# Grouped-query decode attention on one core: the second of the last four value pieces loaded by five loads of 112, 5, 5, 3 and 3 partitions in place of one of 128

## The chip, the core and the metric

The kernel runs on one core of one Trainium2 chip. Its time is the device time of one execution in microseconds (us). The kernel before takes 628.2 us, the median of three runs that lie between 628.05 and 628.32 us. The engines are named as in the profile: PE is TensorE (PEld its weight loads), DVE VectorE, ACT ScalarE, POOL GpSimd and SP SyncE. SP does no arithmetic here; it issues the loads. Behind it stand the core's 16 DMA engines, which carry the bytes. In this document "engine" alone, where loads are spoken of, means one of those 16.

## The reference

Thirty-two query heads attend to 65,536 keys; four query heads share one of eight key and value heads. There is one query per head and the head size is 128, all in bf16:

```python
B, Hq, Hkv, Sq, Sk, D = 1, 32, 8, 1, 65536, 128

def reference(q, k, v):
    rep = Hq // Hkv
    k = jnp.repeat(k, rep, axis=1)
    v = jnp.repeat(v, rep, axis=1)
    scale = D ** -0.5
    scores = jnp.einsum("bhqd,bhkd->bhqk", q, k) * scale
    p = _softmax(scores, axis=-1)
    return jnp.einsum("bhqk,bhkd->bhqd", p, v)
```

Keys and values are 134 MB each, and every byte is used once.

## The kernel before

**Tiling.** The key and value rows of a head are cut into two halves, so there are 16 rounds (NR) of 8 MB of keys and 8 MB of values. In a round, each of the 128 partitions holds 256 row tiles of 128 numbers (2T = 256), so that one load of a whole round's values has 128 rows of 64 KB. `vbuf` holds one round's values. A round is computed in two parts, of A = 160 and C = 96 row tiles.

**The compute loop.** PE turns each key tile (line 139), DVE or ACT copies eight of them out of PSUM (lines 246 and 248), and PE multiplies them by the queries into scores (line 157). DVE takes the largest score, POOL spreads it over the partitions, ACT makes the exponentials (line 416), and PE multiplies them by the value tiles (`stretch`, line 183): one matmul a row tile, accumulated in PSUM. In an odd round, `stretch` runs over the row tiles in the order 96 to 159 (`q` = 1), 160 to 255 (`q` = 2) and 0 to 95 (`q` = 0). The rescaling of the running sums is done on DVE (lines 319 and 322).

**The loads.** SP issues all loads of keys and values on one queue in the order of use: keys of a round when `kfree` says that the key buffer is free, values when `vfree` does. A whole round's load is one DMA, and its completion adds 16 to a semaphore. The loop in the middle loads one DMA for keys and one for values a round. The last round is cut finer, so that PE can begin before all of it has landed: its keys come in three loads, and its values in five. First come row tiles 96 to 255 (semaphore `vrdy[0]`), then row tiles 0 to 95 in four pieces of 62, 22, 9 and 3 row tiles (`V_PIECES`), each with a semaphore of its own in `vpiece`. These four are the "last four value pieces".

**The waits on them.** In `stretch` with `q` = 0 the matmul that starts a piece (row tiles 0, 62, 84 and 93) waits for its semaphore. That code is one loop for all rounds, so the waits are also met in the earlier rounds, where the pieces don't exist: SP adds 16 to each of the four at the start, no wait takes anything off, and SP takes the 16 off again just ahead of the last round's value loads.

**The end.** After the last matmul of the last stretch, DVE adds the partial sum (line 322), PE turns the sum (line 215), DVE and ACT divide it (lines 402 and 439), and SP stores the last head's four rows (line 517). The other 28 rows are stored a little earlier by ACT's queue (line 438).

Of the kernel before, what the change touches and what calls it, by code (L numbers as in the profile page):

```python
# [10 lines left out]
P = 128  # L11
# [13 lines left out]
HU = 4  # L25

V_PIECES = (62, 22, 9, 3)

LOOP_SLOT = 0

# [11 lines left out]
def take(e, sem, n=1):  # L42

    e.wait_ge(sem, n)
    e.sem_inc(sem, -n)  # L45


def bass_standalone__gqa_softmax__decode_kernel(nc, q, k, v, out):
# [14 lines left out]
    def row_tile(odd, x):  # L63
        return (x + C) % (2 * T) if odd else x
# [6 lines left out]
    def sb(name, shape, dt):  # L71
        return S(nc.sbuf_tensor(name, shape, dt))

    def sem(name):
        return S(nc.semaphore(name))

    kbuf = sb("kbuf", [P, (2 * T + C) * D], DT.bfloat16)
    vbuf = sb("vbuf", [P, 2 * T * D], DT.bfloat16)
# [38 lines left out]
    vrdy = [sem(f"vrdy{i}") for i in range(2)]  # L117
    vpiece = [sem(f"vpiece{i}") for i in range(len(V_PIECES))]
    kfree, vfree = sem("kfree"), sem("vfree")
# [59 lines left out]
    def stretch(pe, q):  # L179
        a, b = ((0, C), (C, A), (A, 2 * T))[q]  # L180
        starts = [sum(V_PIECES[:n]) for n in range(len(V_PIECES))] if q == 0 else []
        for r in range(a, b):
            ins = pe.matmul(vsum[q], lhsT=vbuf[:, r * D:(r + 1) * D], rhs=pts[:, r * R:(r + 1) * R],  # L183
                            start=r == a, stop=r == b - 1)
            if r in starts:
                ins.wait_op(vpiece[starts.index(r)], 16, "sem-ge")
        return ins

    def pe_values(pe, n):

        with pe.If(n > 0):
            take(pe, vrdy[0], 16)
            take(pe, exd)
            stretch(pe, 1)


        odd = (n + 1) % 2  # L200
        with pe.Fori(odd, 2) as s:
            with pe.If(n > 0):
                with pe.If(s > 0):
                    take(pe, vrdy[1], 16)
                    take(pe, exd)
                    stretch(pe, 2).then_inc(pvd, 1)
            with pe.If(n > 0):
                with pe.If((n + 1 + s) % 2 < 1):
                    take(pe, exd)
                    stretch(pe, 0).then_inc(pvd, 1)  # L210
# [248 lines left out]
    def pairs(x):  # L459

        return x.rearrange("h (c p t) d -> (h c) p (t d)", c=HALVES, p=P)

    def sync_engine(e):
        kp, vp = pairs(kf), pairs(vf)

        def cols(a, b):
            return slice(a * D, b * D)

        def load_k(i, odd, split=(0,)):

            for n, f in enumerate(split):
                last = (split + (len(K_PARTS),))[n + 1]
                a, b = K_PARTS[f], (K_PARTS + (2 * T,))[last]
                r = row_tile(odd, a) if b - a < 2 * T else 0
                t = r if odd else C + r
                e.dma_start(kbuf[:, cols(t, t + b - a)], kp[i][:, cols(r, r + b - a)]).then_inc(krdy[f], 16)
                for x in range(f + 1, last):
                    e.sem_inc(krdy[x], 16)

        def load_v(i, ready, a, b):  # L480
            e.dma_start(vbuf[:, cols(a, b)], vp[i][:, cols(a, b)]).then_inc(ready, 16)

        def load_both(i, odd):
            take(e, kfree)
            load_k(i, odd)
            take(e, vfree)
            load_v(i, vrdy[0], 0, 2 * T)
            e.sem_inc(vrdy[1], 16)

        load_k(0, 0, (0, 1, 2))  # L490
        load_v(0, vrdy[0], 0, 2 * T)

        for sm in [vrdy[1]] + vpiece:
            e.sem_inc(sm, 16)
        load_both(1, 1)
        with e.Fori(1, H - 1) as h:
            load_both(2 * h, 0)
            load_both(2 * h + 1, 1)
        i = NR - 2
        take(e, kfree)  # L500
        load_k(i, 0, (0, 2))
        take(e, vfree)
        load_v(i, vrdy[0], 0, A)
        load_v(i, vrdy[1], A, 2 * T)
        i = NR - 1
        take(e, kfree)
        load_k(i, 1, (0, 1, 2))
        take(e, vfree)
        for sm in vpiece:
            e.sem_inc(sm, -16)  # L510
        load_v(i, vrdy[0], C, 2 * T)
        e.sem_inc(vrdy[1], 16)
        r = 0
        for n, sm in zip(V_PIECES, vpiece):
            load_v(i, sm, r, r + n)
            r += n
        ins = e.dma_start(of[HR - R:HR, :].rearrange("(a b) d -> a b d", a=2), olast[:, :])
        ins.wait_op(t_last, 2, "sem-ge")
        ins.then_inc(o_sem, 16)
# [4 lines left out]
    scalar_engine(nc.scalar)  # L524
    gpsimd_engine(nc.gpsimd)
    sync_engine(nc.sync)
    nc.sync.wait_ge(o_sem, 32)
    es.close()
# [27 lines left out]
```

## Time and profile before

| | |
|---|---|
| median of three runs | 628.2 us (628.05 to 628.32) |
| the profiled execution, as timed | 628.48 us |
| its span, first to last instruction | 627.2 us |
| granted TensorE clock, mean over the span | 0.768 |
| HBM read | 268.44 MB |
| busy: PE, DVE, ACT, POOL | 78%, 45%, 38%, 3% |

The span is what the profile's rows are placed in; the 1.3 us between it and the 628.48 us lie around the first and the last instruction. Times in the rows are microseconds from the span's start, unless they are marked ns. A row of the timeline reads: start, duration, engine, line, operation, what is written from what, and how many instructions were merged into it. In a table of windows, each row is a stretch of time with the busy time of every engine, the count of instructions in brackets, the granted clock, the busy share of the 16 DMA engines and the rate.

### The profile page before, as it was taken

The page shows a single profiled execution, that of the slowest core. Times are in us where ns is not written, and L with a number is a line of the kernel's source. Part 1 is how long each engine was busy: PE and PEld are TensorE (multiplying, and loading weights), DVE is VectorE, ACT ScalarE, POOL GpSimd, SP SyncE. Part 2 cuts the span into 40 slices and gives each one's busy share as a digit, 9 for nine tenths or more (in the row PEclk, how much of TensorE's full clock was granted, in tenths as well). Part 3 has the DMA queues.
Part 4 walks back from the last instruction along what each step waited for, and adds up shares of the span by engine and source line. Part 5 has one row for each costly group of instructions (what it writes and reads, how often), then busy time and mean ns, then how long its engine had stood idle before and what let it go on. Part 6 is the DMA issues. An engine that isn't in the chain of part 4 may idle for free. (4 is left out here: it accounts for less than half of the span.)

```text
span 627.2 us, 27062 instructions
## 1 busy us (share of the span) xinstructions
PE 486.8 (78%) x12291; PEld 482.8 (77%) x12291; DVE 284.0 (45%) x667; ACT 235.5 (38%) x467; POOL 16.4 (3%) x49
## 2 busy tenths in 40 slices
PE   1873994959859498695976959679496895989898
PEld 1873985959859498694966959679496895989897
DVE  2530553616546065361734617345173552736365
ACT  1330441524425044251533515335052351624354
POOL 0000000000000000000000000000000000000000
PEclk9975875858769587695966959678596785958697
DMA  9999999999999999999999999999999999999997
GB/s 368 439 442 431 435 435 435 431 426 443 426 443 426 439 426 439 426 435 431 431 439 431 439 431 431 439 431 439 431 431 439 431 439 431 412 436 425 432 438 303
DMA packets 6155, 268.59 MB, mean 428 GB/s; under 512 B 770, under 2 KB 898, under 8 KB 1154
## 3 DMA queue, kind: packets, MB, share of 16 engines
q1 hardware_dynamic: 6056, 268.44, 99.2%
q8 instruction: 7, 0.11, 0.1%
q10 hardware_dynamic: 90, 0.02, 0.0%
q14 instruction: 2, 0.02, 0.0%
HBM read 268.44 MB, written 0.01 MB: 428 GB/s over the span
## 5 line engine op out<-in xcount | busy, mean ns | idle before, releaser
L139 PE MATMUL trb<-ident,kbuf 128*128 128x128 bf16 x4096 | 299.8, 236 | 111.3 <-PEq L45 105.3
L139 PEld LDWEIGHTS trb<-ident,kbuf 128*128 128x128 bf16 x4096 | 268.1, 107 | 112.6 <-issue 111.6
L246 ACT ACTIVATE ktb<-trb 128x1024 bf16<-128x1024 bf16 x176 | 180.1, 1023 | 352.2 <-PE trb L139 345.2
L248 DVE COPY ktb<-trb 128x1024 bf16<-128x1024 bf16 x336 | 221.3, 689 | 170.1 <-PE trb L139 167.3
L157 PE MATMUL qkb<-qcur,ktb 128*128 128x4 bf16 x4096 | 132.1, 164 | 0.0
L157 PEld LDWEIGHTS qkb<-qcur,ktb 128*128 128x128 bf16 x4096 | 124.2, 96 | 0.0
L183 PE MATMUL pvb<-pts,vbuf 128*128 128x4 bf16 x2560 | 71.8, 166 | 11.2 <-PEq L45 11.2
L183 PEld LDWEIGHTS pvb<-pts,vbuf 128*128 128x128 bf16 x2560 | 70.0, 102 | 13.1 <-issue 13.1
L416 ACT ACTIVATE pts<-qkb,negm 128x160 bf16<-128x160 f32 (+1 forms) x128 | 51.9, 548 | 0.0
L283 DVE TENSOR_REDUCE cmax<-qkb 128x4 f32<-128x640 f32 (+1 forms) x32 | 22.1, 691 | 58.8 <-DVEq L45 58.8
L183 PE MATMUL qkb<-pts,vbuf 128*128 128x4 bf16 x1536 | 43.4, 166 | 4.5 <-PEq L45 4.5
L183 PEld LDWEIGHTS qkb<-pts,vbuf 128*128 128x128 bf16 x1536 | 42.4, 104 | 5.0 <-issue 5.0
L416 ACT ACTIVATION_READ_ACCUMULATOR pts<-qkb,negm 128x1 f32 x128 | 34.2, 267 | 0.0
L455 POOL PARTITION_ALL_REDUCE cmaxa<-cmax x32 | 12.0, 375 | 578.0 <-POOLq L45 578.0
L410 ACT ACTIVATE alpha<-dm 128x4 f32<-128x4 f32 x32 | 6.4, 201 | 31.9 <-ACTq L45 31.9
L333 DVE COPY acc<-qkb 128x4 f32<-128x4 f32 x8 | 1.3, 162 | 35.3 <-DVEq L45 35.3
L311 DVE TENSOR_TENSOR lp<-lp,alpha 128x4 f32<-128x4 f32 x24 | 3.9, 162 | 26.8 <-DVEq L45 26.8
L322 DVE TENSOR_TENSOR acc<-acc,pvb 128x4 f32<-128x4 f32 x32 | 5.0, 158 | 22.8 <-DVEq L45 22.0
L223 PE MATMUL trb<-ident,qsb 32*128 32x32 bf16 x1 | 0.2, 179 | 11.5 <-issue 11.5
L223 PEld LDWEIGHTS trb<-ident,qsb 32*128 32x128 bf16 x1 | 0.1, 101 | 11.5 <-issue 11.5
L300 DVE TENSOR_TENSOR m<-m,cmaxa 128x4 f32<-128x4 f32 x24 | 3.8, 159 | 8.8 <-DVEq L45 8.8
L319 DVE TENSOR_TENSOR acc<-acc,alpha 128x4 f32<-128x4 f32 x24 | 3.9, 162 | 4.2 <-DVEq L45 3.7
(45 smaller groups left out, 38.1 us busy)
## 6 DMA issues: line engine op xcount, KB each, us to landing
kbuf<-in_k_dram SPq DMA_DIRECT2D x5, 3072.0 KB, 24.4
vbuf<-in_v_dram SPq DMA_DIRECT2D x2, 5120.0 KB, 22.4
kbuf<-in_k_dram SPq DMA_DIRECT2D x1, 5120.0 KB, 18.6
kbuf<-in_k_dram SPq DMA_DIRECT2D x2, 2048.0 KB, 12.8
vbuf<-in_v_dram SPq DMA_DIRECT2D x1, 3072.0 KB, 27.6
vbuf<-in_v_dram SPq DMA_DIRECT2D x1, 1984.0 KB, 28.3
vbuf<-in_v_dram SPq DMA_DIRECT2D x1, 704.0 KB, 29.6
vbuf<-in_v_dram SPq DMA_DIRECT2D x1, 288.0 KB, 29.9
```

The lines of the kernel that those rows point to most:

```text
L139: ins = pe.transpose(trb[j % NTB][:, i * P:(i + 1) * P], kbuf[:, t * D:(t + 1) * D], ident[:, :])
L157: ins = pe.matmul(bank[:, t * R:(t + 1) * R], lhsT=ktb[:, off:off + P], rhs=qcur[:, :], start=True, stop=True)
L183: ins = pe.matmul(vsum[q], lhsT=vbuf[:, r * D:(r + 1) * D], rhs=pts[:, r * R:(r + 1) * R], start=r == a, stop=r == b - 1)
L246: ins = e.activation(dst, trb[j % NTB][:, :], AF.Copy).then_inc(eva, 1)
L248: ins = e.tensor_copy(dst, trb[j % NTB][:, :]).then_inc(evd, 1)
L283: e.tensor_reduce(cmax[:, :], qkb[part][:, 0:n * R].rearrange("p (t g) -> p g t", g=R), AX.X, ALU.max).then_inc(cm, 1)
L311: chain(e, lambda: e.tensor_tensor(lp[:, :], lp[:, :], alpha[u % 2][:, :], ALU.mult), lambda: e.tensor_tensor(lp[:, :], lp[:, :], rsum[u % ...
L319: return lambda: e.tensor_tensor(acc, acc, alpha[u % 2][:, :], ALU.mult)
L322: return lambda: e.tensor_tensor(acc, acc, vsum[q], ALU.add)
L410: e.activation(alpha[u % 2][:, :], dm[u % 2][:, :], AF.Exp, scale=scale)
L416: ins = e.activation(pv[:, g, r:r + n], sv[:, g, 0:n], AF.Exp, bias=negm[b][:, g:g + 1], scale=scale, accum_out=rsum[b][:, g:g + 1])
L455: e.partition_all_reduce(cmaxa[:, :], cmax[:, :], P, bass.bass_isa.ReduceOp.max).then_inc(cma, 1)
```

## The change

The second piece, 22 row tiles of all 128 partitions, is loaded by five DMAs that share its semaphore: partitions 0 to 111, 112 to 116, 117 to 121, 122 to 124 and 125 to 127. Each adds 16 when it is complete, so that this piece's semaphore stands at 80 when all have landed (`landed`). PE's wait for the piece is for 80, and SP's additions at the start and subtraction before the last round are 80 for it as well. The other three pieces, their order and the bytes are as before.

```diff
 V_PIECES = (62, 22, 9, 3)
+SHARED = 1
+ROWS = ((0, 112), (112, 117), (117, 122), (122, 125), (125, 128))
+
+
+def landed(n):
+    return 16 * (len(ROWS) if n == SHARED else 1)
...
             if r in starts:
-                ins.wait_op(vpiece[starts.index(r)], 16, "sem-ge")
+                ins.wait_op(vpiece[starts.index(r)], landed(starts.index(r)), "sem-ge")
...
-        def load_v(i, ready, a, b):
-            e.dma_start(vbuf[:, cols(a, b)], vp[i][:, cols(a, b)]).then_inc(ready, 16)
+        def load_v(i, ready, a, b, rows=slice(0, P)):
+            e.dma_start(vbuf[rows, cols(a, b)], vp[i][rows, cols(a, b)]).then_inc(ready, 16)
...
-        for sm in [vrdy[1]] + vpiece:
-            e.sem_inc(sm, 16)
+        e.sem_inc(vrdy[1], 16)
+        for n, sm in enumerate(vpiece):
+            e.sem_inc(sm, landed(n))
...
-        for sm in vpiece:
-            e.sem_inc(sm, -16)
+        for n, sm in enumerate(vpiece):
+            e.sem_inc(sm, -landed(n))
         load_v(i, vrdy[0], C, 2 * T)
         e.sem_inc(vrdy[1], 16)
         r = 0
-        for n, sm in zip(V_PIECES, vpiece):
-            load_v(i, sm, r, r + n)
+        for x, (n, sm) in enumerate(zip(V_PIECES, vpiece)):
+            for a, b in ROWS if x == SHARED else ((0, P),):
+                load_v(i, sm, r, r + n, slice(a, b))
             r += n
```

On SP's queue, at the end of its program, the values of the last round stood so before (the size is partitions by numbers in a row; 2816 numbers are the 22 row tiles of the second piece):

```order
L481 DMA vbuf<-in_v_dram 128x20480
L481 DMA vbuf<-in_v_dram 128x7936
L481 DMA vbuf<-in_v_dram 128x2816
L481 DMA vbuf<-in_v_dram 128x1152
L481 DMA vbuf<-in_v_dram 128x384
L517 DMA out_dram<-olast 4x128
```

and stand so now:

```order
L487 DMA vbuf<-in_v_dram 128x20480
L487 DMA vbuf<-in_v_dram 128x7936
L487 DMA vbuf<-in_v_dram 112x2816
L487 DMA vbuf<-in_v_dram 5x2816 x2
L487 DMA vbuf<-in_v_dram 3x2816 x2
L487 DMA vbuf<-in_v_dram 128x1152
L487 DMA vbuf<-in_v_dram 128x384
L525 DMA out_dram<-olast 4x128
```

Four DMAs are new, and the third and fourth pieces are issued behind them. On PE, the last stretch of value matmuls keeps its order and its four waiting instructions; the first row names the wait for the vectors of exponentials and the first piece:

```order
L189 MATMUL qkb<-pts,vbuf 128x4 [waits exd,vpiece0]
L189 MATMUL qkb<-pts,vbuf 128x4 x61
L189 MATMUL qkb<-pts,vbuf 128x4 [waits vpiece1]
L189 MATMUL qkb<-pts,vbuf 128x4 x21
L189 MATMUL qkb<-pts,vbuf 128x4 [waits vpiece2]
L189 MATMUL qkb<-pts,vbuf 128x4 x8
L189 MATMUL qkb<-pts,vbuf 128x4 [waits vpiece3]
L189 MATMUL qkb<-pts,vbuf 128x4 x2
```

These rows read as before but for the line number; only the value waited for at `vpiece1` is another.

## The prediction

> **What bounds the kernel now.** I read the page's counters first, then the chain that ended last, then the last five microseconds in windows.
>
> ```profile
> span 627.2 us, 27062 instructions
> ...
> DMA  9999999999999999999999999999999999999997
> ...
> DMA packets 6155, 268.59 MB, mean 428 GB/s; under 512 B 770, under 2 KB 898, under 8 KB 1154
> ...
> q1 hardware_dynamic: 6056, 268.44, 99.2%
> q8 instruction: 7, 0.11, 0.1%
> q10 hardware_dynamic: 90, 0.02, 0.0%
> ```
>
> The queue of the loads keeps the 16 DMA engines busy for 99.2% of the span, and in all forty slices but the last. So the kernel is bound by its loads, and the change neither adds a byte nor moves one before the last round. Only two things can change the time: when the last bytes land, and how much work is left behind them.
>
> The chain of waits, in order of time, shows what is left:
>
> ```profile
> 619.53 0.04 issue
> 619.58 2.70 PE pvb L183 x96
> 622.28 2.79 PE qkb L183 x96
> 625.07 0.02 issue
> 625.09 0.17 DVE acc L322
> ```
>
> It starts at 619.53 us and is PE's two last stretches, without a stop that the chain would name. PE's own timeline gives the second stretch from its first start, and the table of windows the clock:
>
> ```profile
> 622.16 2.89 PE L183 MATMUL qkb<-pts,vbuf 128*128 128x4 bf16 x96
> ...
> 619.60:620.60 1.00, 1.00 (x39) 1.00 (x40) 0.00 (x0) 0.93 (x6) 0.00 (x0) 0.50 0.94 395
> ...
> 623.20:624.20 1.00, 1.00 (x43) 1.00 (x41) 0.67 (x5) 0.00 (x0) 0.00 (x0) 0.50 0.33 119
> ```
>
> The same 96 matmuls at the same granted clock of 0.50 take 2.70 us in the stretch whose values had long landed and 2.89 us in the one that waits for the four pieces. So 2.89 - 2.70 = 0.19 us is all that the pieces cost PE now. That they cost anything is seen in the issues and their landings (SP's timeline, then the list of issues, whose last number is the time from issue to landing):
>
> ```profile
> 594.14 0.42 SPq L481 DMA_DIRECT2D vbuf<-in_v_dram  x1
> ...
> 594.62 0.90 SPq L481 DMA_DIRECT2D vbuf<-in_v_dram  x2
> ```
>
> ```profile
> vbuf<-in_v_dram SPq DMA_DIRECT2D x1, 704.0 KB, 29.6
> vbuf<-in_v_dram SPq DMA_DIRECT2D x1, 288.0 KB, 29.9
> vbuf<-in_v_dram SPq DMA_DIRECT2D x1, 96.0 KB, 29.7
> ```
>
> The second piece (704 KB) lands at 594.14 + 29.6 = 623.7 us, the third at 594.62 + 29.9 = 624.5, the fourth at 594.62 + 0.45 + 29.7 = 624.8. Left to itself, PE would begin at 622.16 and with 2.70 / 96 = 0.028 us a matmul want row tile 62 at 623.9, 84 at 624.5 and 93 at 624.8. The four pieces are so sized that bytes and PE arrive nearly together. PE ends at 625.05, a quarter of a microsecond behind the last landing.
>
> The DMA engines do not end together, though:
>
> ```profile
> 622.50:622.75 0.25, 0.25 (x16) 0.25 (x13) 0.24 (x2) 0.00 (x0) 0.00 (x0) 0.50 0.78 302
> ...
> 623.50:623.75 0.25, 0.25 (x16) 0.25 (x13) 0.21 (x2) 0.00 (x0) 0.00 (x0) 0.50 0.46 163
> 623.75:624.00 0.25, 0.25 (x14) 0.25 (x12) 0.06 (x1) 0.00 (x0) 0.00 (x0) 0.50 0.23 77
> 624.00:624.25 0.25, 0.25 (x16) 0.25 (x13) 0.16 (x1) 0.00 (x0) 0.00 (x0) 0.50 0.10 29
> ```
>
> The next-to-last number is the busy share of the 16: 0.78, about 12 or 13 engines, at 622.6; 0.46, about seven, at 623.6; 0.23 and 0.10 after that. With equal loads some engines end almost 2 us ahead of others. A piece has landed only when the last of them is done. That is what unequal shares could even out, if the larger shares go to engines that are early.
>
> **The change part by part.** *How a load is shared out.* The trace does not name the engine of a packet, but it counts packets. The two stores and the load of the queries have other numbers of rows than 128. On ACT's queue (q10) the first row below is of the window 590 to 628 us, which holds the store of 28 rows; the second, of the window from 626 us, holds the store of four rows on SP's queue:
>
> ```profile
> q10 hardware_dynamic: 42, 0.01, 0.1%
> ...
> q1 hardware_dynamic: 8, 0.00, 0.5%
> ```
>
> 42 packets are 28 rows and 14 completions; 8 are four rows and four completions; the 90 - 42 = 48 that are left on q10 are the 32 rows of the queries and 16 completions. So 28 rows went to 14 engines by two, four rows to four by one, 32 rows to 16 by two. By that, 112 rows go to 16 engines by seven, five rows to five by one, and three rows to three by one. *Which* engines take the small loads has no row, so I bound it. If the 16 rows fell on 16 different engines, everyone would have eight as before: no change. If all four small loads use the same engines from one end, three engines have 7 + 4 = 11 rows, two have 9, and eleven have 7.
>
> [...]
>
> I take the second end, since a rule that spreads successive small loads evenly would need a memory from load to load, and both stores above show nothing of the kind either way.
>
> *Price of a row.* A row of the piece is 704 KB / 128 = 5.5 KB. The rate in a long undisturbed window:
>
> ```profile
> 300.00:338.70 38.70, 29.29 (x758) 29.12 (x756) 17.80 (x45) 13.95 (x30) 1.19 (x3) 0.74 1.00 434
> ```
>
> 434 / 16 = 27 GB/s an engine, so 5632 bytes take 0.21 us. Eleven engines end their part 0.21 us sooner, two 0.21 us later, three 0.62 us later. Each small load adds a completion packet: the eight packets of the four-row store took 0.5% of 16 engines' 1.2 us, 0.1 us in all or 0.012 us apiece, so four extra are 0.05 us. The last figures are +0.67 us for three engines and about +0.23 us for two. The third and fourth pieces are queued behind, so they shift by the same amounts.
>
> *Price on SP.* Four more issues at about 0.45 us (0.90 us for two, above) keep SP busy until about 595.5 + 1.8 = 597.3 us. The bytes of the pieces are reached some 25 us later, and SP's next work is the store of the last four rows near 626 us, so this is hidden. Without that cover it would cost the 1.8 us. The extra `sem_inc` values and the wait for 80 instead of 16 change no count of instructions on PE, DVE or ACT.
>
> *The sum.* If the late engines are among the eleven, the pieces land at 623.5, 624.3 and 624.6, all ahead of PE's wish. Then PE's stretch shrinks to 2.70 us at the best and what is late next is PE itself: -0.19 us, of which I take -0.15, since each wait instruction keeps some cost. If one of the three is the latest engine now, the last landing goes to 624.8 + 0.67 = 625.5 us and PE's end, a quarter of a microsecond behind it, from 625.05 to 625.7: +0.65 us. These are the ends of the sum. Against the span they make 627.0 and 627.8 us. The profiled execution was timed at 628.48 us, 0.3 us over the median of the runs, so I carry the differences to the median: 628.2 - 0.15 = 628.05 and 628.2 + 0.65 = 628.85 us.
>
> **The rivals.** *(A) The three engines are early: 628.05 us, my forecast.* For it: at 623.6 us only about seven of 16 are still at work, so nine could take 0.67 us more without being last. The queue named "instruction" carried seven packets with 0.11 MB, 16 KB each, 0.6 us of an engine's time each at 27 GB/s; an engine that served one would be behind from then on, and seven is also the number of late ones. If instruction packets and small loads use different ends of the row of engines, A holds. Against it: three drawn at random from 16 are all among nine early ones in only 9/16 x 8/15 x 7/14 = 15% of draws; if the three are neighbours and early ones stand together too, it is nearer one half.
>
> *(B) Slower: one of the three is late, 628.2 + 0.1 to 628.2 + 0.65, in the middle 628.5 us.* This is the same mechanism with the other sign: it decides as soon as one of the three now ends less than 0.67 us ahead of the last one, so that its extra rows set the landing of pieces two to four. The 15% above speak for it, the early majority against it.
>
> *(C) Loads of 112 rows run slower than loads of 128.* Then each engine's seven rows cost up to twice 0.21 us: 2.9 us instead of 1.7, the landing moves by 1.2 us, and the time is 629.4 us. In favour is only that no load of this program has seven rows an engine; against it, that the 28-row and 32-row transfers show nothing odd.
>
> [...]
>
> *(D) A small load goes to one engine whole.* That engine has 7 + 16 = 23 rows, 15 x 0.21 = 3.1 us more, and the time is 631.3 us. The four-row store with its four completions speaks against it.
>
> *(E) The change does not do what it says: the rows end up spread evenly.* Then 628.2 us, with a hundredth or two for completions.
>
> **How the numbers follow.** Three runs before spread over 0.27 us, and no change under 0.2% (1.26 us) counts as one. A 0.48, B 0.37, C 0.07, D 0.03, E 0.05. The likeliest is A, 628.05, which I round to 628.1 us. Its own range is 627.8 to 628.3, by the runs' scatter around it. The whole range must reach across B's ends, 628.0 to 628.85, with that scatter: 627.8 to 628.9 us; C's worst and D are left out. Within 0.2% lie A, B, E and most of C: 0.93. Slower takes D and the rest of C, 0.05; faster than 626.9 us has no mechanism, since PE's 0.19 us are all there is, and I leave it 0.02.
>
> **What would show it.** The list of issues of the changed kernel should show five loads for the second piece, and the packets on SP's queue should grow by 16 completions and no more. For A the busy share of the DMA engines should fall later and steeper (over 0.5 at 623.5 us, near nothing after 624.0), the third and fourth piece should land by 624.3 and 624.6, and PE's last stretch should take 2.70 to 2.75 us. For B that stretch takes 3.0 us or more, with a low share that drags beyond 624.3. For C the share stays at 1 while the rate drops below 400 GB/s around 621 to 622 us. The prediction is wrong if the span changes anywhere ahead of 619.5 us, or if the time moves by more than 1.26 us.

## The result and the profile after

| | before | after |
|---|---|---|
| median of six runs | 628.25 us (628.05 to 628.40) | 630.84 us (630.49 to 631.67) |
| the profiled execution, as timed | 628.48 us | 630.62 us |
| its span | 627.2 us | 629.1 us |

The ratio is 1.0044, with a 95% interval of 1.0034 to 1.0054: the change makes the kernel 2.6 us (0.4%) slower. The forecast was 628.1 us with a range up to 628.9 us.

The page of the kernel after, where the prediction looked first:

```profile
span 629.1 us, 27066 instructions
...
DMA packets 6171, 268.59 MB, mean 427 GB/s; under 512 B 786, under 2 KB 914, under 8 KB 1170
...
q1 hardware_dynamic: 6072, 268.44, 99.2%
```

The queue of the loads has 6072 - 6056 = 16 packets more, all of 4 bytes (692 of them, 676 before): the 5 + 5 + 3 + 3 completions of the small loads. So the rows went to as many engines as the prediction counted, and nothing was added besides. In a long window in the middle the rate is nearly what it was (434 before):

```profile
300.00:338.70 38.70, 29.97 (x782) 29.80 (x780) 18.54 (x46) 15.15 (x30) 1.19 (x3) 0.78 1.00 432
```

The time is lost at the end. The chain that ended last no longer is PE's alone; it hangs on a load:

```profile
592.46 0.27 SPq L487
592.72 0.04 issue
592.76 33.17 DMA vbuf<-in_v_dram
625.93 0.04 issue
625.98 1.08 PE qkb L189 x34
627.06 0.02 issue
627.09 0.17 DVE acc L328
```

PE's timeline shows both places where it stops (in brackets the idle time before, and who ended it):

```profile
619.40 2.70 PE L189 MATMUL pvb<-pts,vbuf 128*128 128x4 bf16 x96 [0.21 <-PEq L51]
623.17 1.81 PE L189 MATMUL qkb<-pts,vbuf 128*128 128x4 bf16 x62 [1.07 <-DMA vbuf<-in_v_dram]
625.98 1.07 PE L189 MATMUL qkb<-pts,vbuf 128*128 128x4 bf16 x34 [1.00 <-DMA vbuf<-in_v_dram]
```

The last stretch, one run of 96 matmuls before, is cut in two. It waits 1.07 us for the first piece, which the change does not touch, and 1.00 us for the second. The third and fourth pieces bring no further stop. The two waits, 1.07 + 1.00 = 2.07 us, are nearly all of the difference of the two profiled executions, 630.62 - 628.48 = 2.14 us.

Windows of the end say what the DMA engines did (the last two numbers are their busy share and the rate in GB/s; a packet is counted whole in the window in which it starts, so a share can pass 1). After the change:

```profile
618.10:619.10 1.00, 1.00 (x41) 1.00 (x38) 0.02 (x1) 0.72 (x6) 0.00 (x0) 0.50 1.08 460
619.10:620.10 1.00, 0.79 (x31) 0.73 (x29) 0.30 (x2) 0.00 (x0) 0.21 (x1) 0.50 0.96 378
620.10:621.10 1.00, 1.00 (x44) 1.00 (x41) 0.78 (x5) 0.00 (x0) 0.22 (x1) 0.50 1.14 289
621.10:622.10 1.00, 1.00 (x38) 0.91 (x35) 0.78 (x5) 0.00 (x0) 0.00 (x0) 0.50 0.80 177
622.10:623.10 1.00, 0.00 (x1) 0.00 (x0) 0.48 (x3) 0.00 (x0) 0.00 (x0) 0.50 0.98 209
623.10:624.10 1.00, 0.93 (x35) 0.94 (x36) 0.00 (x0) 0.00 (x0) 0.00 (x0) 0.50 0.98 207
```

and before:

```profile
619.40:620.40 1.00, 0.82 (x31) 0.85 (x32) 0.00 (x0) 1.00 (x8) 0.00 (x0) 0.50 0.85 355
620.40:621.40 1.00, 1.00 (x44) 1.00 (x42) 0.33 (x2) 0.13 (x2) 0.00 (x0) 0.50 0.93 386
621.40:622.40 1.00, 1.00 (x43) 1.00 (x40) 0.39 (x3) 0.00 (x0) 0.43 (x1) 0.50 1.01 401
```

The row to look at is the one from 622.10 us: a share of 0.98 with 209 GB/s. The engines hold packets nearly all the time and carry about half as much. It is close to what the prediction said would show rival C (a share of 1 and less than 400 GB/s around 621 to 622 us; the row from 621.10 us has 0.80 and 177).

The trace also holds the start, the length and the size of every single packet, and one row of a piece is one packet. A row of the second piece, 5632 bytes, lasted 0.216 us in the median before (0.224 at most) and lasts 0.382 us after (0.646 at most). Of the 128 such packets after, 119 last longer than 0.23 us. The small loads have only 16 of the 128, so at least 103 of the slow ones belong to the 112 rows. This does not yet say why they are slow.

### The profile page after: what moved, and what is told of

Read it like the earlier page. It is cut to its first block, busy times and chain, and to the rows that moved or that the text cites. A ratio compares the mean times of both kernels' runs of the same rounds, so it can differ in the third digit from the quotient of the medians.

```text
span 629.1 us, 27066 instructions
## 1 busy us (share of the span) xinstructions
PE 488.1 (78%) x12291; PEld 483.9 (77%) x12291; DVE 284.3 (45%) x667; ACT 235.8 (37%) x467; POOL 16.5 (3%) x49
## 3 DMA queue, kind: packets, MB, share of 16 engines
q1 hardware_dynamic: 6072, 268.44, 99.2%
## 5 line engine op out<-in xcount | busy, mean ns | idle before, releaser
L229 PE MATMUL trb<-ident,qsb 32*128 32x32 bf16 x1 | 0.2, 181 | 11.6 <-issue 11.6
L229 PEld LDWEIGHTS trb<-ident,qsb 32*128 32x128 bf16 x1 | 0.1, 98 | 11.6 <-issue 11.6
```

## The experiments

Three theories were open. *Partitions*: which destination partitions stand together in a load decides how long its packets last. *Uneven shares*: three engines with 11 rows end last. *Small loads*: loads on three or five engines, or just more loads, cost by themselves. Where an expectation speaks of collisions, it means packets that last longer than those of a load of all 128 partitions (0.216 us for a row of the second piece in the kernel before). All eleven kernels were timed or profiled beside the kernel before, which stood at 628.15 to 628.25 us in each set. A ratio is the time over that of the kernel before, with its 95% interval in brackets.

**1. Two loads, with even shares.** Against the change:

```diff
-ROWS = ((0, 112), (112, 117), (117, 122), (122, 125), (125, 128))
+ROWS = ((0, 112), (112, 128))
```

> The second piece in two loads, of 112 and 16 partitions: seven rows and one row for each of 16 engines, so every engine has eight rows as before and no load uses fewer than 16 engines. [...] Uneven-shares theory (the engines with 11 rows are the late ones): 628.2 to 628.4 us. Small-loads theory (loads on three or five engines cost by themselves): 628.2 to 628.5 us.

Measured: 630.59 us (630.31 to 630.72), ratio 1.0038 [1.0024, 1.0052]. By the prediction's count every engine has eight rows again and no load uses fewer than 16 engines, and nearly all of the loss is still there. Uneven shares and loads on few engines are out as the main cause.

**2. Two halves.** `ROWS = ((0, 64), (64, 128))`.

> The second piece in two loads of 64 partitions each: four rows for each of 16 engines, twice. [...] Uneven-shares and small-loads theories: shares are even and all engines are used, 628.2 to 628.4 us.

Measured: 631.06 us (630.15 to 632.06), ratio 1.0051 [1.0034, 1.0068]. Four rows for each engine, twice, and about the same loss, with a wider spread: it is not the number seven either.

**3. Five loads of all partitions.** The second piece is cut by row tiles instead of partitions:

```diff
+COLS = (14, 2, 2, 2, 2)
...
-            for a, b in ROWS if x == SHARED else ((0, P),):
-                load_v(i, sm, r, r + n, slice(a, b))
-            r += n
+            for c in COLS if x == SHARED else (n,):
+                load_v(i, sm, r, r + c)
+                r += c
```

> [...] A theory that the number of loads, of packets or of completions costs: 629 to 631 us.

Measured: 628.55 us (628.46 to 628.65), ratio 1.0006 [0.9996, 1.0015]. It has five loads and more and smaller packets than the change. It is 0.35 us over the kernel before (628.20 us), and its runs all lie above those of that kernel (highest 628.40), though the interval of the ratio holds 1. So the number of loads explains about 0.35 us of the 2.6 us, if anything, and is not the main cause.

**4. The same cut far from the end.** The kernel before, with the first round's values in two loads, of which SP waits after it has issued the next keys:

```diff
-        load_v(0, vrdy[0], 0, 2 * T)
+        e.dma_start(vbuf[0:112, :], vp[0][0:112, :]).then_inc(first, 16)
+        e.dma_start(vbuf[112:128, :], vp[0][112:128, :]).then_inc(first, 16)
...
+        load_k(1, 1)
+        e.wait_ge(first, 32)
```

> The kernel before, with the values of the first round loaded in two loads of 112 and 16 partitions, far from the end; the last round is as before. [...] Theories on uneven shares or small loads at the end: the rate stays at 430 and the time at 628 to 628.5 us.

Measured: 651.68 us (651.02 to 652.01), ratio 1.0376 [1.0359, 1.0393]. That is 23.5 us over the kernel before, with the last round as it was. Three windows of it:

```profile
25.00:30.00 5.00, 2.05 (x40) 1.96 (x38) 1.34 (x2) 0.72 (x1) 0.00 (x0) 0.84 0.95 213
30.00:35.00 5.00, 2.02 (x74) 1.93 (x71) 0.82 (x1) 1.02 (x1) 0.37 (x1) 0.50 0.90 210
...
55.00:60.00 5.00, 0.00 (x0) 0.00 (x0) 0.33 (x2) 0.00 (x0) 0.00 (x0) 0.50 0.36 43
```

The kernel before has 419 and 410 GB/s from 25 to 30 and 30 to 35 us. The 7.3 MB of 112 rows at 211 instead of 415 GB/s are 35 - 18 = 17 us. The rest falls to the load of 16 neighbouring rows (43 GB/s, third row): its 16 packets of 64 KB last 8.1 to 9.8 us each, where a row of 64 KB takes 2.42 us in the median in the loads of 128 rows.

**5. Loads alone.** Ahead of the kernel before, twelve loads of 64 KB rows, each issued when the one before has landed. One shows the form:

```diff
+        e.dma_start(vbuf[0:128:2, :], vp[0][0:64, :]).then_inc(alone, 16)
+        take(e, alone, 16)
```

> Ahead of the kernel before stand twelve loads of 64 KB rows into the value buffer, each alone and waited for (what they bring is overwritten later); the whole grows by 150 to 300 us, and the time from issue to landing of each is what counts. At 27 GB/s an engine a row takes 2.4 us, and about 2 us pass for a load as such. If only the rows of each engine count: 128 rows 21 us, 120 rows (15 engines) 21, 112 rows 19, 96 rows 17, 64 rows 12 wherever they go, 32 rows 7, 16 rows 4.5 wherever they go, 5 rows 4.5. [...] Source theory (the rows in memory collide, not the partitions): the loads with the same source rows agree, and the ones with spread source rows differ from them.

SP's timeline gives each issue; the next issue is the landing and about 0.1 us:

```profile
0.73 0.41 SPq L491 DMA_DIRECT2D vbuf<-in_v_dram  x1
24.16 0.41 SPq L493 DMA_DIRECT2D vbuf<-in_v_dram  x1
66.79 0.33 SPq L495 DMA_DIRECT2D vbuf<-in_v_dram  x1
99.22 0.31 SPq L497 DMA_DIRECT2D vbuf<-in_v_dram  x1
131.33 0.57 SPq L499 DMA_DIRECT2D vbuf<-in_v_dram  x1
154.33 0.49 SPq L501 DMA_DIRECT2D vbuf<-in_v_dram  x1
166.74 0.47 SPq L503 DMA_DIRECT2D vbuf<-in_v_dram  x1
189.72 0.32 SPq L505 DMA_DIRECT2D vbuf<-in_v_dram  x1
201.95 0.32 SPq L507 DMA_DIRECT2D vbuf<-in_v_dram  x1
213.55 0.53 SPq L509 DMA_DIRECT2D vbuf<-in_v_dram  x1
221.25 0.31 SPq L511 DMA_DIRECT2D vbuf<-in_v_dram  x1
233.00 0.26 SPq L513 DMA_DIRECT2D vbuf<-in_v_dram  x1
244.10 1.30 SPq L477 DMA_DIRECT2D kbuf<-in_k_dram  x3
```

The differences stand in the table, each timed once, beside the median length of a load's packets and what the rows of the busiest engine would take at 2.42 us each, the median packet of the 128 rows. Up to 245 us SP's queue has 913 packets, 733 rows and 180 completions; 180 is the count with 15 completions for the 120 rows, five for the five and 16 for each of the others, and by it the rows are divided in the last column:

| to partitions | from rows | measured, us | median packet, us | rows of an engine x 2.42 us |
|---|---|---|---|---|
| 0 to 127 | same | 23.4 | 2.42 | 19.4 |
| 0 to 119 | same | 42.6 | 5.11 | 19.4 |
| 0 to 111 | same | 32.4 | 4.55 | 16.9 |
| 0 to 95 | same | 32.1 | 4.95 | 14.5 |
| 0 to 63 | 0 to 63 | 23.0 | 5.12 | 9.7 |
| 0 to 126, every second | 0 to 63 | 12.4 | 2.42 | 9.7 |
| 0 to 63 | 0 to 126, every second | 23.0 | 5.12 | 9.7 |
| 0 to 31 | same | 12.2 | 5.12 | 4.8 |
| 0 to 15 | 0 to 15 | 11.6 | 8.63 | 2.4 |
| 0 to 120, every eighth | 0 to 15 | 7.7 | 4.78 | 2.4 |
| 0 to 15 | 0 to 120, every eighth | 11.7 | 8.51 | 2.4 |
| 0 to 4 | same | 11.1 | 7.91 | 2.4 |

Two pairs decide it. 64 rows to neighbouring partitions take 23.0 us and the *same source rows* to every second partition 12.4 us; spreading the source instead changes nothing (23.0). With 16 rows it is 11.6, 7.7 and 11.7 us, and the packets say the same. So with the same number of rows the destination partitions set the pace, and not the memory that is read. 112 rows take 9 us longer than 128, and 120 rows 19 us longer.

Over the time of its rows' packets a load took 4.0 us (128 rows, 23.4 - 8 x 2.42), 2.7 us (every second partition, 12.4 - 4 x 2.42) and 2.0 us (32 rows, 12.2 - 2 x 5.12), where the expectation has about 2. The loads of neighbours are slow by their packets: 5.12 us a row in the load of 64, 8.63 in that of 16 and 7.91 in that of five, against 2.42 in the load of 128. What holds a packet up no view shows, and so it stays open why the loads of 96, 112 and 120 rows, with no more rows for an engine than the load of 128, take 32.1, 32.4 and 42.6 us.

**6. Two halves, even and odd partitions.** `ROWS = ((0, 128, 2), (1, 128, 2))`, as slices with a step.

> The second piece in two loads of 64 partitions, the even ones and the odd ones. In the loads measured alone, 64 neighbouring partitions took 22.9 us and 64 partitions two apart 12.3 us. [...] A theory that any cut of the piece by partitions costs: 630 us or more.

Measured: 628.18 us (628.05 to 628.46), ratio 1.0000 [0.9991, 1.0009]. The same bytes, the same number of loads and the same four rows for each engine as experiment 2, and 2.9 us less. PE's last stretch is whole again (first row). From 622 to 623 us the share of the DMA engines is the same in experiment 2 (second row) and here (third row), and the rate is not:

```profile
622.24 2.79 PE L189 MATMUL qkb<-pts,vbuf 128*128 128x4 bf16 x96
...
622.00:623.00 1.00, 0.30 (x12) 0.27 (x11) 0.52 (x4) 0.00 (x0) 0.00 (x0) 0.50 0.97 220
...
622.00:623.00 1.00, 1.00 (x43) 1.00 (x41) 0.62 (x5) 0.00 (x0) 0.00 (x0) 0.50 0.97 378
```

A row of the second piece lasts 0.361 us in the median in experiment 2 and 0.215 us here.

This settles the main cause of the loss: it is which partitions stand together in a load.

**7 and 8. The small loads on top of a whole piece.** The second piece is one load of 128 partitions; behind it come four loads of 5, 5, 3 and 3 rows into a tile that nobody reads (16 rows more than the computation needs), first of partitions 20 apart, then of the partitions that the change has:

```diff
+MORE = ((0, 100, 20), (4, 104, 20), (8, 68, 20), (68, 128, 20))
...
+            load_v(i, sm, r, r + n)
+            for part in MORE if x == SHARED else ():
+                w = slice(*part)
+                e.dma_start(spare[w, 0:n * D], vp[i][w, cols(r, r + n)]).then_inc(sm, 16)
```

The other has `MORE = ((112, 117), (117, 122), (122, 125), (125, 128))`.

> [...] The engines that take the small loads have 8 + 4 = 12 rows. If they are early ones (rival A of the prediction): 628.2 to 628.6 us. If one of them is among the late ones (rival B): 4 x 0.21 = 0.85 us later, 628.8 to 629.3 us. If small loads cost by themselves: 630 us or more.

> As the kernel with the small loads 20 partitions apart, but the small loads take partitions 112 to 127, neighbours, as in the change; the rows, the engines and the counts are the same. [...] If partitions do not matter: the same time as that kernel.

Measured: 628.86 us (628.63 to 629.39), ratio 1.0012 [1.0003, 1.0022], and 629.26 us (629.11 to 629.68), ratio 1.0018 [1.0009, 1.0027]. Neighbours cost 0.4 us more than spread rows, in medians whose ranges overlap a little. The first number was to tell rival A from rival B. It lies in the range set for B, and yet it does not decide: packets of 5632 bytes last 0.246 us on the mean in that kernel and up to 0.355, against 0.218 and 0.224 in the kernel before, so packets are slowed in it too, and how its 0.7 us divide stays open.

**9 and 10. The change's shares without its block.** The even partitions in one load and the odd ones in loads of 48, 5, 5, 3 and 3, or of 48 and 16:

```diff
+ROWS = ((0, 128, 2), (1, 97, 2), (97, 107, 2), (107, 117, 2), (117, 123, 2), (123, 128, 2))
...
+ROWS = ((0, 128, 2), (1, 97, 2), (97, 128, 2))
```

> The shares of the change without its block of neighbours: the second piece in six loads, of the 64 even partitions, 48 odd ones (1 to 95) and the odd ones from 97 on in loads of 5, 5, 3 and 3. By counts of rows, three engines have 4 + 3 + 4 = 11 rows, two have 9 and eleven have 7, as in the change. [...] With rival B (one of them is late): 628.5 to 629.0 us. If the collisions are not what the change costs: 630.5 us or more.

> The same but with the last 16 odd partitions in one load, one row for each of 16 engines, so that all have eight rows. [...] The difference to the kernel with unequal shares is what the shares do by themselves: below zero for rival A, 0.3 us or more for rival B.

Measured: 629.98 us (629.61 to 630.22), ratio 1.0027 [1.0017, 1.0037], and 629.66 us (629.34 to 630.11), ratio 1.0023 [1.0014, 1.0032]. The first expectation missed: the time lies between the range of B and the 630.5 us set for another cause. The second kernel, with even shares, is 1.5 us over the kernel before (628.20 us). It looks as if a load of 48 odd partitions slows packets although one of 64 does not. A window of the kernel with even shares, with the mark of it:

```profile
621.00:622.00 1.00, 0.94 (x36) 0.85 (x32) 0.47 (x3) 0.00 (x0) 0.43 (x1) 0.50 0.92 167
```

In the single packets the 39 that start first, from 619.45 us on, last at most 0.226 us. An engine with four even rows, three of the 48 and one of the 16 can't reach the last before 619.45 + 7 x 0.215 = 620.96 us, and 13 packets longer than 0.23 us start before that. So, with the rows shared as counted, the slow packets begin with the load of 48. How its rows are dealt to the engines no view shows. Unequal shares come out 0.3 us above even ones, which is the side of B, but with ranges that overlap and slow packets in both, so this pair leaves A and B open as well.

**11. Extra rows that touch no partition.** The kernel before, with the four small loads of experiment 8 (the same `MORE`) behind the second piece as copies from memory to memory; no stretch waits for them:

```diff
             load_v(i, sm, r, r + n)
+            for a, b in MORE if n == 22 else ():
+                e.dma_start(away[a:b, :], vp[i][a:b, cols(r, r + n)]).then_inc(aside, 16)
```

> The kernel before, with four loads of 5, 5, 3 and 3 rows of 5.5 KB queued behind the second piece that copy the rows to another place in memory and touch no partition; nothing waits for them but the end of the program. [...]

Measured: 628.31 us (628.15 to 628.63) beside 628.15, ratio 1.0001 [0.9992, 1.0010]. PE's last stretch and the chain's end:

```profile
621.85 2.38 PE L186 MATMUL qkb<-pts,vbuf 128*128 128x4 bf16 x84
624.58 0.48 PE L186 MATMUL qkb<-pts,vbuf 128*128 128x4 bf16 x12 [0.35 <-DMA vbuf<-in_v_dram]
```

This is nearer to A than to B. At the prediction's price, B asks for 4 x 0.21 = 0.85 us more at the end, and A for none. The time stands 0.16 us over the kernel before, and packets of 5632 bytes last 0.217 us on the mean (0.218 before). The last packet of the values ends at 624.36 us against 624.24, so of the 0.85 us 0.12 came, and one profile of each can't tell 0.12 us from scatter. PE waits 0.35 us for the third piece, but it had begun the stretch 0.31 us earlier than before (621.85 against 622.16). The end of the stretch is where it was, at 624.58 + 0.48 = 625.06 us against 625.05. At 0.217 us a row, the change's shares (three rows more, not four, and one less for the eleven) would hardly have moved the time; that is an estimate from this run.

No kernel that was run beats the kernel before.

## Why the prediction was wrong

*What bounds the kernel* held: PE's last two stretches and the landings of the four pieces set the end, and the rate in the middle is nearly the same (432 GB/s against 434). The time moved by 2.6 us, more than the 1.26 us that the prediction named as a sign of being wrong.

*How a load is shared out* held as far as it can be seen: 16 packets more, all of them completions.

*The price of a row* is the step that failed. The prediction took 434 / 16 = 27 GB/s an engine from loads of 128 partitions and used it for loads of any shape: "so 5632 bytes take 0.21 us". That price is right for the kernel before (0.216 us), for even and odd halves (0.215) and in experiment 11 (0.215). In the change a row takes 0.382 us in the median. All terms of the sum, -0.21, +0.23 and +0.67 us, stood on that one number, and so did the choice between A and B. The sum also put at nothing what the new loads do to the loads around them. That all four small loads use the same engines, on which +0.67 and +0.23 us rest as well, was the author's choice and no run shows it; experiment 11, with four loads of the same rows that touch no partition, stands 0.16 us over the kernel before. Nor does a run show the cost of a wait for which 0.04 of the 0.19 us were kept: in the kernel before, the same stretch two rounds earlier (from 554.80 us), whose four waits were met long ahead, took 2.70 us at the same clock of 0.50, as long as the 96 matmuls ahead of it that wait for no piece.

*Rival A* gained nothing that could show, and *rival B* was a second-order question: experiment 11 stands 0.16 us over the kernel before, which its interval does not tell from none. Which engines took the small loads stays open. *Rival E*, no change at all, is excluded by the time itself.

*Rival C* named what happened, loads of 112 rows that run slower, with a chance of 0.07 and too small a price: 629.4 us. It doubled the price of the seven rows, 1.2 us, and stopped there. For the second piece that was nearly right: an estimate from its packets is 8 x (0.381 - 0.218) = 1.3 us an engine, with the means after and before. What it left out are the loads around it. By the same working the first piece costs 0.3 us more (0.632 against 0.596 us a row), the third 0.5 (0.152 against 0.095) and the fourth 0.1 (0.048 against 0.036). That makes 2.2 us in all, and the last packet of the values ends 2.0 us later (626.25 us against 624.24).

So the first piece, though unchanged, comes late as well: PE waits 1.07 us for it in the change and 1.02 and 0.70 us in experiments 1 and 2, and not at all in experiment 6, where a row of the piece behind it lasts 0.215 us. In the change, packets of the second piece start from 619.47 us on, while the last of the first piece starts at 620.98; the longest packet of the first piece lasts 1.03 us there and 0.60 before. The argument against C, that the transfers of 28 and 32 rows showed nothing odd, was empty: their rows are 256 bytes and last at most 0.022 us, too short a time to tell.

Measured alone, C's own claim holds: 112 rows took 32.4 us, 128 rows 23.4. Why the packets of such a load last longer (4.55 against 2.42 us in the median) no view shows.

*Rival D* ends near the measured time, at 631.3 us, by accident: the count of completions excludes it, and in experiment 1 no small load of that kind exists. *SP's issues* show no cost of their own: in the change SP has issued the last of the values at 593.9 us, and experiment 3, with four more issues as well, stands 0.35 us over the kernel before, if that is its own.

## What to carry to other kernels

A load's price is also a property of its destination partitions, and not of its bytes alone: before a load of all 128 partitions is cut by partitions, measure the piece by itself, since 64 neighbours can take as long as 128 (23.0 and 23.4 us alone). A cut into even and odd partitions kept the time (experiment 6), and cutting each row into five cost 0.35 us or nothing (experiment 3). And a busy share of 1 does not say that the engines run at their rate; read the GB/s beside it (0.98 with 209 GB/s here, against 401 at 1.01 before).

## What was not expected of the hardware

Loads that leave out a few partitions can be slower than whole ones in absolute time: 120 rows 42.6 us, 112 rows 32.4 us, 128 rows 23.4 us. Five rows to five neighbouring partitions took 11.1 us, nearly as long as 16 (11.6 us). The cost also spreads to transfers of all 128 partitions that are in flight at the same time (0.60 us a packet at most before, up to 1.03 us in the change's first piece). And spreading a load over partitions is no cure by itself: 64 odd partitions behind the 64 even ones ran at full rate, 48 odd ones did not, and no run here explains why.
